# Fused attention with a gelu gate on one core: six output adds moved to GpSimd, another block order near the end, tail tasks by priority, and the last 128 queries scored in two parts of 64

## The chip, the cores and the metric

One core of a Trainium2 chip runs the whole kernel. The metric is device time in microseconds (us) of one launch. In all runs here but one it is the span of the profile plus about 1.83 us (483.73 at a span of 481.9), so spans can be used for sums.

## The reference, cut to what matters

```python
B, S, D = 1, 2048, 448             # 16 heads of 28 columns; F = 1792
xn = _layernorm(x, axis=-1)
scores = jnp.einsum("bhqd,bhkd->bhqk", q, k) * 28 ** -0.5
p = _softmax(scores, axis=-1)
s = jnp.einsum("bhqk,bhkd->bhqd", p, v).reshape(B, S, D) @ wo
g = _silu(_gelu(xn @ w1 + b1) @ w2 + b2)
return x + s * g
```

## The kernel before

The kernel has no fixed order of instructions in its text. Every operation is a task with an engine, a modelled duration and a priority; a scheduler that runs while the program is built picks, engine by engine, the next task and writes it into that engine's queue.

The work is 16 blocks: four groups of heads by four chunks of 512 queries. Within a block, TensorE forms a tile of scores (128 keys by 512 queries for one head, into the PSUM buffer `ring`), ScalarE takes its exponential into `P`, and TensorE multiplies `P` by the values into `acc`. ScalarE exponentiates three tiles at a time (1536 columns), sometimes two (1024): then VectorE computes the third, a **late tile**, with a polynomial.

```python
yield _Task(DVE, lambda eng: eng.tensor_scalar(v, lo, EXP_SC / 65536.0, None, op0=ALU.mult), ty, [tv], d0, 0.0, 4)
yield _Task(DVE, lambda eng: eng.scalar_tensor_tensor(u, v, EXP_A, v, op0=ALU.add, op1=ALU.mult),
            [tv], [tu], d1, 0.0, 4)
# ... two more steps on u and v ...
yield _Task(DVE, lambda eng: eng.scalar_tensor_tensor(pl.bitcast(dt.uint16), y, 2.0 ** -9, u,
                                                      op0=ALU.mult, op1=ALU.add),
            ty + [tu], [K.b_pl[k]], d1, 0.0, 4)          # the late tile, for TensorE
```

The five steps are L1297, L1298, L1300, L1302, L1304 before the change and L1310, L1311, L1313, L1315, L1317 after it. TensorE's value product of a late tile stands in TensorE's fixed order; if the polynomial is not done, everything behind it waits, the next scores too.

When all four groups of a chunk are done, its four output tiles of 128 queries are projected, multiplied by the gate out of PSUM and added to x:

```python
def t_oev(self, ps, tok, c, t):
    ...
    yield _Task(DVE, lambda eng: eng.tensor_tensor(o, ps, K.g_sb[:, c, t, :], ALU.mult), ..., [wr], 0.63, 0.0, 3)
    yield _Task(DVE, lambda eng: eng.tensor_tensor(o, o, K.x2[:, c, t, :], ALU.add),
                [K.b_x2[c], wr], [wr], 0.4, 0.0, 3)
```

The gate of the very last tile is made after the last exponential, on GpSimd:

```python
yield _Task(POOL, lambda eng: eng.tensor_tensor(o, sg[:, 3, :], fb[:, 3, :], ALU.mult), ..., 0.85, 0.05, 0)
yield _Task(POOL, lambda eng: eng.tensor_tensor(o, o, fb[:, 3, :], ALU.add), ..., 0.85, 0.05, 0)
```

## Time and profile before

| | before |
|---|---|
| time, median of 3 | 483.76 us (483.73 to 483.79) |
| span of the profiled run, its own time | 483.1, 484.9 us |
| exponentials of 1536 / 1024 columns on ScalarE | 249 / 100 |
| last exponential's end to last add's end | 4.47 us |
| GpSimd busy | 43.2 us (9%) |

### The profile page before, as it was taken

Reading aid. Unit: us, or ns where it says so; the run is one execution under the profiler, and the core shown is the slowest. Engines: PE = TensorE matmul, PEld = TensorE weight load, DVE = VectorE, ACT = ScalarE, POOL = GpSimd, SP = SyncE. Lnnn points to the kernel's source line nnn. Section 1 sums busy time; section 2 is a strip of 40 time slices with the busy share of each in tenths; the row PEclk is TensorE's granted clock in tenths of the full one; section 3 lists DMA queues with packets and bytes.
Section 4 is the critical chain, followed back from the end, with each engine's and each line's share of the span. In section 5 each row is a group of like instructions: output and inputs, shape, how many; then the busy total and the mean of one; then the engine's idle time right before and its main releaser. Section 6 shows DMA issues by size and latency. Waiting matters only on the chain.

```text
span 483.1 us, 10155 instructions
## 1 busy us (share of the span) xinstructions
PE 438.5 (91%) x4232; PEld 168.1 (35%) x4268; DVE 407.6 (84%) x592; ACT 468.8 (97%) x390; POOL 43.2 (9%) x77
## 2 busy tenths in 40 slices
PE   6999899998889898999989988999999999999995
PEld 5442333332223333332323343333333333333453
DVE  8946888989978989989878749899997999889785
ACT  5999999999999999999999999999999999999994
POOL 7470000000010000000101000010100100100001
PEclk9998999999999999999999999999999999999998
DMA  8501000000000000000400000000101010011011
GB/s 247 149 9 28 1 0 2 1 2 2 0 1 1 1 1 1 1 2 1 134 1 0 1 2 0 1 2 1 38 1 40 1 38 1 23 37 58 3 39 39
DMA packets 8288, 11.08 MB, mean 23 GB/s; under 512 B 1650, under 2 KB 6898, under 8 KB 8243
## 3 DMA queue, kind: packets, MB, share of 16 engines
q1 hardware_dynamic: 8098, 10.21, 7.0%
q8 instruction: 33, 0.54, 0.5%
q10 hardware_dynamic: 144, 0.23, 0.1%
q14 instruction: 13, 0.10, 0.1%
HBM read 8.61 MB, written 1.84 MB: 22 GB/s over the span
## 4 chain that ended last, share of the span: by engine, by line
ACT 45%; PE 32%; issue 17%; DVE 5%; ACTq 0%; DVEq 0%
ACT P L1160 42%; PE ring L1129 9%; PE acc L1346 6%; PE misc L1065 4%; PE acc L857 3%; PE misc L695 2%; ACT h L1044 2%; PE misc L1007 1%; PE acc L839 1%; PE misc L949 1%; PE misc L1442 1%; PE ring L1007 1%; ACT w L1080 1%; PE ring L949 1%; DVE kT L1298 0%
## 5 line engine op out<-in xcount | busy, mean ns | idle before, releaser
L1160 ACT ACTIVATE P<-ring 128x1536 bf16<-128x1536 f32 (+1 forms) x350 | 428.9, 1469 | 1.7 <-PE ring L1129 1.5
L1129 PE MATMUL ring<-qT,kT 32*128 32x512 bf16 (+2 forms) x1144 | 136.5, 360 | 26.1 <-ACT P L1160 22.0
L1346 PE MATMUL acc<-P,vaug 128*32 128x512 bf16 (+2 forms) x1074 | 95.0, 363 | 1.0 <-issue 0.5
L1129 PEld LDWEIGHTS ring<-qT,kT 32*128 32x128 bf16 x1144 | 35.5, 91 | 132.8 <-ACT P L1160 123.5
L1183 DVE TENSOR_SCALAR x_sb<-ring 128x512 int32<-128x512 f32 x68 | 46.8, 688 | 14.2 <-PE ring L1129 13.0
L1065 PE MATMUL misc<-w,h 128*128 128x448 bf16 x224 | 52.3, 355 | 0.1
L1415 POOL CAST rhi<-rc 128x16 bf16<-128x16 f32 x15 | 10.3, 686 | 402.5 <-DVE rc L1413 255.6
L857 PE MATMUL acc<-ident,zero 128*128 128x128 bf16 x516 | 44.8, 221 | 0.0
L1346 PEld LDWEIGHTS acc<-P,vaug 128*32 128x32 bf16 x1074 | 24.4, 93 | 51.0 <-issue 46.6
L857 PEld LDWEIGHTS acc<-ident,zero 128*128 128x128 bf16 x516 | 29.8, 98 | 21.3 <-issue 19.4
L1007 PE MATMUL misc<-xnT,w 128*128 128x512 bf16 x127 | 35.9, 382 | 1.3 <-issue 0.8
L990 DVE CAST h<-misc 128x512 bf16<-128x512 f32 x35 | 24.1, 688 | 8.1 <-PE misc L1007 7.0
L1304 DVE SCALAR_TENSOR_TENSOR x_sb<-x_sb,kT 128x1024 uint16<-128x1024 int32 (+1 forms) x24 | 26.7, 1111 | 0.5
L1302 DVE SCALAR_TENSOR_TENSOR kT<-kT 128x1024 f32<-128x1024 f32 (+1 forms) x24 | 26.6, 1110 | 0.5
L1298 DVE SCALAR_TENSOR_TENSOR kT<-kT 128x1024 f32<-128x1024 f32 (+1 forms) x24 | 26.5, 1104 | 0.6
L1300 DVE SCALAR_TENSOR_TENSOR kT<-kT 128x1024 f32<-128x1024 f32 (+1 forms) x24 | 26.4, 1102 | 0.2
L1065 PEld LDWEIGHTS misc<-w,h 128*128 128x128 bf16 x224 | 17.3, 97 | 23.9 <-issue 12.1
L1007 PE MATMUL ring<-xnT,w 128*128 128x512 bf16 x82 | 19.3, 380 | 2.0 <-ACT h L1044 1.6
L1298 DVE SCALAR_TENSOR_TENSOR w<-w 128x1024 f32<-128x1024 f32 (+1 forms) x18 | 20.3, 1128 | 0.3
L1304 DVE SCALAR_TENSOR_TENSOR x_sb<-x_sb,w 128x1024 uint16<-128x1024 int32 (+1 forms) x18 | 20.3, 1130 | 0.2
L1300 DVE SCALAR_TENSOR_TENSOR w<-w 128x1024 f32<-128x1024 f32 (+1 forms) x18 | 20.3, 1130 | 0.2
L1302 DVE SCALAR_TENSOR_TENSOR w<-w 128x1024 f32<-128x1024 f32 (+1 forms) x18 | 20.3, 1129 | 0.1
(154 smaller groups left out, 449.6 us busy)
## 6 DMA issues: line engine op xcount, KB each, us to landing
h<-in_A_x_dram SPq DMA_DIRECT2D x4, 448.0 KB, 3.3
w<-in_B_w_dram SPq DMA_DIRECT2D x1, 1568.0 KB, 7.3
x_sb<-in_A_x_dram SPq DMA_DIRECT2D x3, 448.0 KB, 5.2
w<-in_B_w_dram SPq DMA_DIRECT2D x1, 1344.0 KB, 9.4
out_dram<-h SPq DMA_DIRECT2D x6, 224.0 KB, 1.9
h<-in_A_wqkv_dram SPq DMA_DIRECT2D x3, 168.0 KB, 5.5
out_dram<-h SPq DMA_DIRECT2D x4, 112.0 KB, 1.7
wo<-in_A_wo_dram SPq DMA_DIRECT2D x16, 24.5 KB
```

Of the source, the lines that this page charges most:

```text
L857: ins = eng.matmul(K.acc[:, 0:128], K.zero[:, :], K.ident[:, :], start=False, stop=True, skip_group_check=True)
L990: yield _Task(DVE, lambda eng: eng.tensor_copy(dst, bank), [tok], wr, 0.69, 0.0, 2)
L1007: ins = eng.matmul(bank, K.w1[:, kt, ft * 128:(ft + 1) * 128], K.xnT[:, kt, c * 512:(c + 1) * 512], start=(kt == 0), stop=(kt == KT - 1))
L1065: ins = eng.matmul(ps, hv[:, ft, t * 128:(t + 1) * 128], K.w2[:, ft, :], start=(ft == 0), stop=(ft == FT - 1))
L1129: return eng.matmul(K.ring[:, RB[m], col:col + nq], K.kT[32 * j:32 * j + 32, g, t * 128:(t + 1) * 128], K.qT[32 * j:32 * j + 32, g, c * 51 ...
L1160: return eng.activation(K.P[:, p0:p0 + n, :], K.ring[:, b0:b0 + n, :], ACTF.Exp, scale=SM_SCALE)
L1183: yield _Task(DVE, lambda eng, m=m, i=i, half=half: eng.tensor_scalar(K.ysb[i][:, 512 * half:512 * half + 512], K.ring[:, RB[m], :], SM_SC ...
L1298: yield _Task(DVE, lambda eng: eng.scalar_tensor_tensor(u, v, EXP_A, v, op0=ALU.add, op1=ALU.mult), [tv], [tu], d1, 0.0, 4)
L1300: yield _Task(DVE, lambda eng: eng.scalar_tensor_tensor(u, u, EXP_B, u, op0=ALU.add, op1=ALU.mult), [tu], [tu], d1, 0.0, 4)
L1302: yield _Task(DVE, lambda eng: eng.scalar_tensor_tensor(u, v, EXP_D, u, op0=ALU.mult, op1=ALU.add), [tv, tu], [tu], d1, 0.0, 4)
L1304: yield _Task(DVE, lambda eng: eng.scalar_tensor_tensor(pl.bitcast(dt.uint16), y, 2.0 ** -9, u, op0=ALU.mult, op1=ALU.add), ty + [tu], [K. ...
L1346: return eng.matmul(K.acc[32 * j:32 * j + 32, q0:q0 + nq], K.vaug[:, t, 4 * g + j, :], ap[:, col:col + nq], tile_position=(0, 32 * j), sta ...
```

## The change

The intent is to empty the end. The last two blocks are both on the last chunk, so that the outputs of chunk 2 are finished a block earlier; six output adds go from VectorE to the idle GpSimd, and the gate's last add the other way; the last 128 queries are handled as two parts of 64; in the tail the scheduler looks ahead for tasks of higher priority. Small matmuls weigh less in the scheduler's count of TensorE activity, and the thresholds for late tiles were tuned again.

```diff
+GC = [(b // C, b % C) for b in range(11)] + [(3, 0), (3, 1), (3, 2), (2, 3), (3, 3)]
-THS = (..., 8.0, 8.0, 8.0, 7.0, 3.0)
+THS = (..., 7.0, 8.0, 4.0, 9.0, 3.0)
+PARTS = [(0, 128), (128, 128), (256, 128), (384, 64), (448, 64)]
+TAIL = 18
+POOL_ADD = 8
...
+            if self.exp_m >= MTOT - TAIL and E in (PE, DVE):
+                for s2, p2 in sorted(((c[0], c[1]) for c in cand), key=lambda c: c[0]):
+                    if p2[3].E == E and p2[3].prio < p[3].prio and s2 < s + p[3].dur - 0.1:
+                        s, p = s2, p2
+                        break
...
-            yield _Task(POOL, lambda eng: eng.tensor_tensor(o, o, fb[:, 3, :], ALU.add),
+            yield _Task(DVE, lambda eng: eng.tensor_tensor(o, o, fb[:, 3, :], ALU.add),
...
-        yield _Task(DVE, lambda eng: eng.tensor_tensor(o, o, K.x2[:, c, t, :], ALU.add),
-                    [K.b_x2[c], wr], [wr], 0.4, 0.0, 3)
+        E, dur = (POOL, 1.05) if POOL_ADD <= 4 * c + t < 14 else (DVE, 0.4)
+        yield _Task(E, lambda eng: eng.tensor_tensor(o, o, K.x2[:, c, t, :], ALU.add),
+                    [K.b_x2[c], wr], [wr], dur, 0.0, pr)
```

(Cut: the pieces of 64 queries, weights 0.15 and 0.3 of small matmuls, the holding back of filler matmuls before a block's copy, priorities.)

More of the change, by code (lines that the diff above doesn't have):

```diff
@@ L47 @@
 LATE_GAP, LATE_SUB = 3, 15
-THS = (8.0, 4.0, 7.0, 8.0, 4.0, 7.0, 9.0, 6.0, 6.0, 8.0, 8.0, 8.0, 8.0, 8.0, 7.0, 3.0)
-SLACKS = (6.0, 5.0, 3.0, 5.0, 2.0, 6.5, 9.0, 6.5, 3.0, 4.0, 7.0, 6.0, 8.0, 6.0, 8.0, 3.0)
+THS = (8.0, 4.0, 7.0, 8.0, 4.0, 7.0, 9.0, 6.0, 6.0, 8.0, 8.0, 7.0, 8.0, 4.0, 9.0, 3.0)
+SLACKS = (6.0, 5.0, 3.0, 5.0, 2.0, 6.5, 9.0, 6.5, 2.0, 4.0, 7.0, 6.0, 8.0, 6.0, 8.0, 3.0)
 NU = len(UNITS)
@@ L83 @@
 class _Task:
-    __slots__ = ("E", "fn", "reads", "writes", "dur", "lat", "rank")
+    __slots__ = ("E", "fn", "reads", "writes", "dur", "lat", "rank", "w")
     @property
@@ L88, in prio, with __init__ @@
         return self.rank() if callable(self.rank) else self.rank
-    def __init__(self, E, fn, reads=(), writes=(), dur=0.1, lat=0.05, prio=5):
+    def __init__(self, E, fn, reads=(), writes=(), dur=0.1, lat=0.05, prio=5, w=1.0):
         self.E, self.fn, self.reads, self.writes = E, fn, list(reads), list(writes)
-        self.dur, self.lat, self.rank = dur, lat, prio
+        self.dur, self.lat, self.rank, self.w = dur, lat, prio, w
 class _Kernel:
@@ L111, in __init__ @@
         self.pe_hist = deque()
+        self.hold = False
     def sem(self, name):
@@ L171, in put @@
         if t.E == PE:
-            self.pe_hist.append((start, start + t.dur))
+            self.pe_hist.append((start, start + t.dur * t.w))
         return h
@@ L223, in run @@
                     s = self.start_of(p[3])
-                    if s is not None:
+                    if s is not None and not (self.hold and p[3].E == PE and p[3].prio >= 90):
                         cand.append((s, p))
@@ L368, in alloc @@
         self.b_selb = B()
-        self.b_E4, self.b_on4, self.b_o4 = ([B() for _ in range(4)] for _ in range(3))
+        self.b_E4, self.b_on4, self.b_o4 = ([B() for _ in range(5)] for _ in range(3))
         self.b_rf = [B(), B()]
-        self.b_sig3, self.b_g3 = B(), B()
+        self.b_sig3, self.b_g3, self.b_g3m = B(), B(), B()
         self.banks = [(self.misc[:, :], self.b_misc), (self.acc[:, :], self.b_acc)]
@@ L403, in schedule @@
         K.late = set(MLATE)
-        K.late_left = [len([m for m in MLATE if K.sub_of(m) == b]) for b in range(NBLK + 3)]
+        K.late_left = [len([m for m in MLATE if K.sub_of(m) == b]) for b in range(NBLK + 4)]
         K.late_q = deque()
@@ L879, in f @@
             return ins
-        yield _Task(PE, f, K.b_wsq[g0:g1] + [K.b_pads], [tok], 0.15 * n + 0.1, 0.1, pr)
+        yield _Task(PE, f, K.b_wsq[g0:g1] + [K.b_pads], [tok], 0.15 * n + 0.1, 0.1, pr, 0.15)
         for b in K.b_hf[1]:
@@ L1093, in p_silu @@
             yield _Task(ACT, lambda eng: eng.activation(sg[:, 3, :], fb[:, 3, :], ACTF.Tanh, scale=0.5),
-                        [K.b_fsb[c % 2]], [K.b_sig3], 0.47, 0.0, 0)
+                        [K.b_fsb[c % 2]], [K.b_sig3], 0.87, 0.0, 0)
             yield _Task(POOL, lambda eng: eng.tensor_tensor(o, sg[:, 3, :], fb[:, 3, :], ALU.mult),
-                        [K.b_sig3, K.b_fsb[c % 2]], [K.b_h[c], K.b_g3], 0.85, 0.05, 0)
-            yield _Task(POOL, lambda eng: eng.tensor_tensor(o, o, fb[:, 3, :], ALU.add),
-                        [K.b_fsb[c % 2]], [K.b_h[c], K.b_g3], 0.85, 0.05, 0)
+                        [K.b_sig3, K.b_fsb[c % 2]], [K.b_h[c], K.b_g3m], 1.03, 0.05, 0)
+            yield _Task(DVE, lambda eng: eng.tensor_tensor(o, o, fb[:, 3, :], ALU.add),
+                        [K.b_fsb[c % 2], K.b_g3m], [K.b_h[c], K.b_g3], 0.4, 0.0, 0)
     def pieces(self, m):
@@ L1105, in pieces @@
             return b, r % 4, [(2 * (r // 4) + k, 0, 256, 256 * k) for k in range(2)], r == 31, 0
-        s, r = r // 16 - 1, r % 16
-        return b, r % 4, [(4 * (r // 4) + k, 128 * (s + 1), 128, 128 * k) for k in range(4)], r == 15, s
+        if r < 48:
+            r -= 32
+            return b, r % 4, [(4 * (r // 4) + k, 256, 128, 128 * k) for k in range(4)], r == 15, 1
+        s, r = (r - 32) // 8, r % 8
+        return b, r % 4, [(8 * (r // 4) + k, 256 + 64 * s, 64, 64 * k) for k in range(8)], r == 7, s
     def p_take(self, b):
@@ L1120, in p_scores @@
             ps = [(m,) + K.pieces(m) for m in ms]
-            for k in range(4):
+            for k in range(8):
                 for m, b, j, pc, _, _ in ps:
@@ L1125, in p_scores @@
                     t, q0, nq, col = pc[k]
-                    g, c = b // C, b % C
+                    g, c = GC[b]
                     def f(eng, m=m, t=t, j=j, g=g, c=c, q0=q0, nq=nq, col=col):
@@ L1268, in p_mlate @@
                 b, j, pc, _, _ = K.pieces(m)
-                t, g, c = pc[0][0], b // C, b % C
+                t, (g, c) = pc[0][0], GC[b]
                 yield _Task(PE, lambda eng, j=j, g=g, t=t, c=c, bank=bank: eng.matmul(
@@ L1336, in p_pv @@
             fl, rd = [], []
-            for kk in range(4):
+            for kk in range(8):
                 for m, ap, tok in src:
                     _, j, pc, _, s = K.pieces(m)
-                    g = q // 16 // C
+                    g = GC[q // 16][0]
                     if kk >= len(pc):
@@ L1366, in p_pv @@
             if end:
+                K.hold = True
                 K.spawn(K.p_epi(b) if b < NBLK - 1 else K.p_epi4(first - NBLK + 1), 0.5)
@@ L1374, in p_epi4 @@
         K = self
-        ts = ((0, 1), (2,), (3,))[s]
-        sl = slice(128 * ts[0], 128 * (ts[-1] + 1))
+        ts = ((0, 1), (2,), (3,), (4,))[s]
+        sl = slice(PARTS[ts[0]][0], sum(PARTS[ts[-1]]))
         yield _Task(DVE, lambda eng: eng.tensor_copy(K.E_sb[:, 1, sl], K.acc[:, sl]), [K.b_acc, K.b_E[1]],
-                    [K.b_E4[t] for t in ts], 0.16 + 0.13 * len(ts), 0.0, 0)
+                    [K.b_E4[t] for t in ts], 0.16 + 0.00105 * (sl.stop - sl.start), 0.0, 0)
         K.E_done = NBLK - 1 + s
+        K.hold = False
         for t in ts:
@@ L1385, in p_norm4 @@
         g, c = G - 1, C - 1
-        E, tE = K.E_sb[:, 1, 128 * t:128 * (t + 1)], K.b_E4[t]
+        q0, n = PARTS[t]
+        E, tE = K.E_sb[:, 1, q0:q0 + n], K.b_E4[t]
         bank, tok = yield ("bank", lambda: K.g_done[C - 1])
-        yield _Task(PE, lambda eng: eng.matmul(bank[:, 0:128], K.selb[:, :], E, start=True, stop=True),
-                    [tE, K.b_selb], [tok], 0.1, 0.12, 3)
-        R = K.rf[:, t % 2, :]
-        yield _Task(DVE, lambda eng: eng.reciprocal(R, bank[:, 0:128]), [tok], [K.b_rf[t % 2]], 0.96, 0.0, 1)
+        yield _Task(PE, lambda eng: eng.matmul(bank[:, 0:n], K.selb[:, :], E, start=True, stop=True),
+                    [tE, K.b_selb], [tok], 0.1, 0.12, 2 if t < 3 else 0)
+        R = K.rf[:, t % 2, 0:n]
+        yield _Task(DVE, lambda eng: eng.reciprocal(R, bank[:, 0:n]), [tok], [K.b_rf[t % 2]], 0.12 + 0.0066 * n, 0.0,
+                    1 if t < 3 else 0)
         K.banks.append((bank, tok))
-        dst = K.qT[:, g, c * 512 + 128 * t:c * 512 + 128 * (t + 1)]
+        dst = K.qT[:, g, c * 512 + q0:c * 512 + q0 + n]
         yield _Task(DVE, lambda eng: eng.tensor_tensor(dst, E, R, ALU.mult), [tE, K.b_rf[t % 2], K.b_qT[g][c]],
-                    [K.b_on4[t]], 0.3, 0.0, 1)
-        K.on4[t] = True
+                    [K.b_on4[t]], 0.16 + 0.00105 * n, 0.0, 1 if t < 3 else 0)
+        if t != 3:
+            K.on4[min(t, 3)] = True
     def p_epi(self, b):
         K = self
-        g, c = b // C, b % C
+        g, c = GC[b]
         E = K.E_sb[:, b % 2, :]
@@ L1404, in p_epi @@
         K.E_done = b
+        K.hold = False
         bank, tok = yield ("bank", lambda: K.ready([tE], 0.2))
@@ L1411, in f @@
             return ins
-        yield _Task(PE, f, [tE, K.b_bsel], [tok], 0.25, 0.1, 3)
+        yield _Task(PE, f, [tE, K.b_bsel], [tok], 0.25, 0.1, 3, 0.3)
         yield _Task(DVE, lambda eng: eng.reciprocal(K.rc[:, :], bank[:, 0:16]), [tok], [K.b_rc], 0.26, 0.0, 1)
@@ L1444, in f @@
             return ins
-        return _Task(PE, f, [K.b_wo] + [K.b_on4[t] if (g, c) == (G - 1, C - 1) else K.b_onT[g][c] for g in gs], [tok], 0.2 * len(gs) + 0.05, 0.12, prio)
+        return _Task(PE, f, [K.b_wo] + [x for g in gs for x in (([K.b_on4[t]] + K.b_on4[4:] * (t == 3)) if (g, c) == (G - 1, C - 1) else [K.b_onT[g][c]])], [tok], 0.2 * len(gs) + 0.05, 0.12, prio)
     def t_oev(self, ps, tok, c, t):
@@ L1449, in t_oev @@
         o = K.osb[:, c, t, :]
+        pr = 3 if (c, t) != (C - 1, 3) else 0
         wr = K.b_osb[c][t // 2] if c < C - 1 else K.b_o4[t]
         yield _Task(DVE, lambda eng: eng.tensor_tensor(o, ps, K.g_sb[:, c, t, :], ALU.mult),
-                    [tok, K.b_g3 if (c, t) == (C - 1, 3) else K.b_g[c]], [wr], 0.63, 0.0, 3)
-        yield _Task(DVE, lambda eng: eng.tensor_tensor(o, o, K.x2[:, c, t, :], ALU.add),
-                    [K.b_x2[c], wr], [wr], 0.4, 0.0, 3)
+                    [tok, K.b_g3 if (c, t) == (C - 1, 3) else K.b_g[c]], [wr], 0.63, 0.0, pr)
+        E, dur = (POOL, 1.05) if POOL_ADD <= 4 * c + t < 14 else (DVE, 0.4)
+        yield _Task(E, lambda eng: eng.tensor_tensor(o, o, K.x2[:, c, t, :], ALU.add),
+                    [K.b_x2[c], wr], [wr], dur, 0.0, pr)
         ov = K.out[0].rearrange("(c p t) d -> c p t d", p=128, t=4)[c]
@@ L1463, in p_out @@
         K = self
-        bank, tok = yield ("bank", lambda: K.on_done[(G - 1) * C + c] and K.g_done[c])
+        bank, tok = yield ("bank", lambda: K.on_done[GC.index((G - 1, c))] and K.g_done[c])
         ps = bank[:, 0:D]
@@ L1476, in p_last @@
         ps = bank[:, 0:D]
-        yield K.t_wo(ps, tok, c, t, (0, 1, 2), 3)
+        for g in range(G - 1):
+            yield K.t_wo(ps, tok, c, t, (g,), 3)
         yield ("until", lambda: K.on4[t])
-        yield K.t_wo(ps, tok, c, t, (3,), 3)
+        yield K.t_wo(ps, tok, c, t, (3,), 3 if t < 3 else 1)
         yield from K.t_oev(ps, tok, c, t)
```

## The prediction

> **What bounds the kernel now.** I read the page first (busy shares, then the forty slices), then ScalarE's groups by shape, then the stretches in which ScalarE was not full, then the timeline of the end. ScalarE is the bound: 97% busy, and in the slices it shows 9 from the second to the last but one.
>
> ```profile
> PE 438.5 (91%) x4232; PEld 168.1 (35%) x4268; DVE 407.6 (84%) x592; ACT 468.8 (97%) x390; POOL 43.2 (9%) x77
> ...
> ACT  5999999999999999999999999999999999999994
> ...
> PEclk9998999999999999999999999999999999999998
> ...
> L1160 ACT ACTIVATE P<-ring 128x1536 bf16<-128x1536 f32 (+1 forms) x350 | 428.9, 1469 | 1.7 <-PE ring L1129 1.5
> ```
>
> So a shorter time can come from three places only: less work on ScalarE, the 1.7 us in which its exponentials waited, and the ends (13 us before the first exponential, and everything after the last). The clock row has one 8 inside the body, in the fourth slice. Stretches of 1 us there show why: the granted TensorE clock is 0.50 for about 3.4 us, and ScalarE falls to 0.16 us busy out of 1.
>
> ```profile
> 42.00:43.00 1.00, 1.00 (x10) 0.30 (x8) 0.57 (x1) 1.00 (x2) 0.00 (x0) 1.00 0.00 0
> 43.00:44.00 1.00, 0.81 (x5) 0.13 (x2) 0.18 (x1) 1.00 (x2) 0.00 (x0) 0.59 0.06 16
> ...
> 45.00:46.00 1.00, 1.00 (x6) 0.11 (x4) 0.73 (x2) 0.89 (x1) 0.00 (x0) 0.50 0.00 0
> 46.00:47.00 1.00, 1.00 (x10) 0.28 (x7) 0.51 (x1) 0.16 (x1) 0.00 (x0) 0.70 0.00 0
> ```
>
> (Columns: stretch, its length, busy us of PE, PEld, DVE, ACT, POOL, then the clock.) The timeline has the victim: two projection matmuls take 1.03 us where the same two take 0.60 at 35.8 us, the scores behind them come late, and ScalarE waits 0.96 us.
>
> ```profile
> 44.75 1.03 PE L695 MATMUL misc<-xnT,wq 128*128 128x512 bf16 x2
> ...
> 46.84 2.79 ACT L1160 ACTIVATE P<-ring 128x1536 bf16<-128x1536 f32 x2 [0.96 <-PE ring L1129]
> ```
>
> The end, in the timeline: the last exponential (892 ns, starting at 475.57) is done at 476.46; call that A. The values product starts at A+0.24 behind three output matmuls, and the last DVE add ends at 480.93 = A+4.47; 2.17 us later the span ends (store, landing 1.7).
>
> ```profile
> 476.70 0.41 PE L1346 MATMUL acc<-P,vaug 128*32 128x128 bf16 x16
> ...
> 477.16 0.29 DVE L1377 CAST E_sb<-acc 128x128 bf16<-128x128 f32 x1 [0.27 <-PE acc L1346]
> 477.44 0.63 DVE L1451 TENSOR_TENSOR h<-ring,h 128x448 bf16<-128x448 f32 x1
> ...
> 478.06 0.96 DVE L1391 RECIPROCAL w<-ring 128x128 f32<-128x128 f32 x1
> ...
> 480.54 0.39 DVE L1453 TENSOR_TENSOR h<-h 128x448 bf16<-128x448 bf16 x1
> ```
>
> The eviction at 477.44 belongs to the tile before; the reciprocal starts 0.61 us after the accumulator copy, where the path alone needs about 0.30 (0.05 to PE, 0.22 matmul, 0.03 back).
>
> **What the Trainium skill says.** "TensorE: Matmul & The Clock Gate", section "What's actually happening": the clock is halved after a window of 3413 ns with too little activity, and restored after a busy one. The trace agrees: 0.50 from about 43.2 to 46.6, one window. Same page, "Wait — 56ns, not 53.3ns?": starts are never closer than about 25 ns, however small the matmul. This trace differs where four tiles run side by side: 32 value products of 128 columns end 0.63 us after they began, 0.22 of it latency, so 13 ns each. "VectorE: DVE Perf Modes", errata section: a fixed cost per instruction. It agrees in form: the copies take 425 ns for 256 columns and 292 for 128, so 1.04 ns a column over 159 fixed. "GPSIMD Engine Reference", 4.1: two-input operations are about twice slower than on VectorE. Here 1.03 against 0.39 us.
>
> **The change, part by part**, counted in the built order of both kernels.
>
> *Clock weights.* The scheduler adds idle-filling matmuls (three of 128 columns, 0.17 us) when it thinks PE is idle. It counted twelve one-column matmuls at 40.7 us as full work. Now they weigh 0.15, and two fillers stand just before the bad window's end, one after the small matmul at 41.44 and one before the projection at 43.24. In the window 39.76 to 43.18 the timeline has seven groups of 512 columns (side by side or alone, each 0.21 us of streaming at the 13 ns per 128 columns in four tiles that is worked out above): 1.5 us of 3.42; two fillers make 1.85. By the same count other windows with 1.6 kept the full clock (around 186 and 289 us), so I give 0.7 that the dip goes. Worth: the waits 0.96 + 0.04, and 0.09 because an exponential that follows at once starts before the one before it has ended. In all −1.05.
>
> *ScalarE's work.* VectorE takes one late tile fewer (67 against 68), so ScalarE gets one exponential of 1536 columns in place of one of 1024. The pitch of 1536 is 1.34 us, the scheduler's and the trace's step per 512 columns 0.43: +0.43, on the path.
>
> *Order of blocks.* The block of the third head group on the last chunk now comes last but one, so all outputs of chunk 2 move a block earlier: four matmuls and 1.02 us of VectorE each. Both engines have room there, ScalarE does not wait for them: 0 by itself. Six adds move from VectorE (0.39) to GpSimd (1.03): off the path, 0. Twelve fillers fewer: 0.
>
> *64-query parts.* 128 score and 128 value matmuls of 64 columns replace 64 and 64 of 128. A unit of scores becomes 24 matmuls in place of 12: at 13 ns or so, +0.2 us. It must be ready within 1.34 us of its release, with at most about 0.9 us of other PE work between: 0.4 before, some 0.65 now, hidden.
>
> *The tail, step by step from A.* One output matmul, not three, stands before the value product, and is long done: start A+0.05. 32 products: 0.63, to A+0.68. Copy of 64 columns 0.23 (159 + 64 × 1.04): 0.70 to 0.93. Sum matmul to 1.20. Reciprocal of 64: from 957 ns at 128 and 248 at 16 columns, 0.55: 1.23 to 1.78. Multiply 0.23 after the 0.10 seen before: 1.88 to 2.11. Output matmul 2.16 to 2.53; the gate's add, now on VectorE, fits below it (its GpSimd half ends near A+1.6). Eviction 2.55 to 3.18, its add to 3.60. But in the built order the previous tile's add stands after that, and so does its store: to A+3.96. Against 4.47 that is −0.51; I take −0.48, as two stores now leave 0.39 us apart.
>
> Sum: 483.76 − 1.05 + 0.43 − 0.48 = 482.66, say 482.7.
>
> **Rivals.** (1) *The dip stays or moves.* For: the fillers are small, and a re-ordered body can open another poor window. Against: the sum above, and no other dip in the body now. Then 483.76 + 0.43 − 0.48 = 483.7, no gain. (2) *PE becomes the bound in the last blocks*, if 64-column matmuls run at the page's 25 ns: a unit would take 0.6 and the last products 0.8 us. Scores would still be hidden, the tail would lose 0.3 to 0.4: 483.0. (3) *VectorE sets the end*: if the deferred add cost nothing (its store hidden), 482.3. If VectorE arrives late at the late tiles of the last block, ScalarE waits: it has about 1 us of slack there, so I hold it unlikely. (4) *New waits of ScalarE* around the moved output work: the largest PE backlog between two score units falls from 2.61 to 1.92 us by my count, which speaks against it.
>
> **Range and chances.** 0.7 for about 482.6 and 0.3 for about 483.7 (rival 1), each within some 0.4. Range 481.9 to 483.9. 2% is 9.7 us, more than all that is not ScalarE's work between first and last exponential: within 2% 0.98.
>
> **What would show it.** Clock 1.00 between 42 and 47 us and no wait of 0.96 before that exponential (clock step). 250 exponentials of 1536 and 99 of 1024 (work). Last exponential's end near 475.8. From it to the last add 3.9 to 4.0 us, the last two DVE instructions adds of 0.39. A copy of 0.23 and reciprocals near 0.55. It is wrong if the clock is 0.50 there, if a new dip or a wait of ScalarE over 0.3 us appears after 300 us, or if the last products take over 0.8 us.

## More of the kernel before

The model lets an engine's task depend on data, never on what another engine does meanwhile.

The profiled run took 484.9 us, 1.1 more than any timed run: what its trace shows need not be in the times. And one line of the groups, with GpSimd's smallest operation, has a mean of 686 ns for 16 columns (columns: busy us, mean ns, idle time before and what ended it):

```profile
L1415 POOL CAST rhi<-rc 128x16 bf16<-128x16 f32 x15 | 10.3, 686 | 402.5 <-DVE rc L1413 255.6 <-PE ring L1129 82.5 <-PE acc L1346 37.9
```

One by one these casts take from 196 to 1085 ns. The same work with the same shape, five times as long at times: something outside the instruction stretches it. (In the trace the long ones are those that start beside a step of the polynomial, as at 237.35, 1085 ns beside L1298; the short ones have no such neighbour.)

## The result, and the profile after

| | before | after |
|---|---|---|
| time, median | 483.75 us (483.66 to 483.79, 4 runs) | 488.07 us (488.33, 488.05, 488.09, 486.58) |
| span of the profiled run | 483.1 | 486.5 |
| exponentials 1536 / 1024 | 249 / 100 | 250 / 99 |
| waits of ScalarE over 0.2 us after 440 us | none | 1.94, 0.26, 0.92 |
| last exponential's end to last add's end | 4.47 | 4.39 |

The ratio is 1.0083 (95% interval 1.0063 to 1.0104). Here and below a ratio is the mean time of one kernel's runs over the mean of the other's in the same rounds, so not quite the ratio of the medians. The time is 4.3 us above before and 4.2 above the top of my range.

The page of the profile, after (share rows, the forty slices, ScalarE's main group):

```profile
PE 438.4 (90%) x4349; PEld 168.1 (35%) x4385; DVE 404.2 (83%) x579; ACT 469.6 (97%) x390; POOL 49.3 (10%) x82
...
ACT  5999999999999999999999999999999999999794
...
PEclk9999999999999999999999999999999999999799
...
L1173 ACT ACTIVATE P<-ring 128x1536 bf16<-128x1536 f32 (+1 forms) x350 | 429.6, 1459 | 4.0 <-PE ring L1142 3.7
```

(POOL 49.3 for 43.2: the adds.) The 8 of the fourth slice in the clock row is gone, and a 7 stands in both rows near the end. The timeline of ScalarE shows which exponentials waited (columns: start, length, then in brackets the idle time before and what ended it):

```profile
455.32 2.86 ACT L1173 ACTIVATE P<-ring 128x1536 bf16<-128x1536 f32 x2 [1.94 <-PE ring L1142]
458.44 1.02 ACT L1173 ACTIVATE P<-ring 128x1024 bf16<-128x1024 f32 x1 [0.26 <-PE ring L1142]
460.38 19.40 ACT L1173 ACTIVATE P<-ring 128x1536 bf16<-128x1536 f32 x15 [0.92 <-PE ring L1142]
```

All three waited for scores, so for TensorE. TensorE's timeline at that place:

```profile
451.23 0.39 PE L1142 MATMUL ring<-qT,kT 32*128 32x256 bf16 x6
453.43 0.44 PE L1359 MATMUL acc<-P,vaug 128*32 128x512 bf16 x4 [1.81 <-DVE x_sb L1317]
```

TensorE stood from 451.62 to 453.43, because the last step of a late tile (L1317) was not done. The stretches of 1 us show what followed (columns: stretch, length, busy us of PE, PEld, DVE, ACT, POOL, clock, DMA share, GB/s):

```profile
452.00:453.00 1.00, 0.00 (x0) 0.00 (x0) 0.97 (x2) 1.00 (x2) 0.00 (x0) 1.00 0.62 229
...
454.00:455.00 1.00, 1.00 (x10) 0.13 (x6) 0.22 (x1) 0.00 (x0) 0.00 (x0) 0.50 0.06 16
```

After that pause TensorE's clock was 0.50 from 453.7 to about 460.5, and six score matmuls took 0.61 us in place of 0.39; I take the 0.26 and 0.92 as the price of that. So the question is why L1317 came late. VectorE's timeline of the changed kernel, and under it GpSimd's (same columns):

```profile
442.70 0.63 DVE L1471 TENSOR_TENSOR h<-misc,h 128x448 bf16<-128x448 f32 x1 [0.99 <-POOL h L1474]
443.24 1.22 DVE L1313 SCALAR_TENSOR_TENSOR kT<-kT 128x1024 f32<-128x1024 f32 x1
444.49 1.94 DVE L1315 SCALAR_TENSOR_TENSOR kT<-kT 128x1024 f32<-128x1024 f32 x1
...
446.88 1.21 DVE L1317 SCALAR_TENSOR_TENSOR x_sb<-x_sb,kT 128x1024 uint16<-128x1024 int32 x1
448.01 1.25 DVE L1310 TENSOR_SCALAR kT<-x_sb 128x512 f32<-128x512 uint16 x1
449.19 0.61 DVE L1471 TENSOR_TENSOR h<-misc,h 128x448 bf16<-128x448 f32 x1
...
450.43 1.40 DVE L1313 SCALAR_TENSOR_TENSOR kT<-kT 128x512 f32<-128x512 f32 x1
...
452.60 0.69 DVE L1317 SCALAR_TENSOR_TENSOR x_sb<-x_sb,kT 128x512 uint16<-128x512 int32 x1
```

```profile
440.71 1.88 POOL L1474 TENSOR_TENSOR h<-h 128x448 bf16<-128x448 bf16 x1 [9.38 <-DVE h L1471]
443.40 1.94 POOL L1474 TENSOR_TENSOR h<-h 128x448 bf16<-128x448 bf16 x1 [0.81 <-DVE h L1471]
447.04 1.94 POOL L1474 TENSOR_TENSOR h<-h 128x448 bf16<-128x448 bf16 x1 [1.69 <-DVE h L1471]
449.88 1.41 POOL L1474 TENSOR_TENSOR h<-h 128x448 bf16<-128x448 bf16 x1 [0.90 <-PE acc L867]
```

Read the two side by side. A GpSimd add takes 1.03 us when it has the memory to itself; these four take 1.41 to 1.94. VectorE's L1315 takes 1.22 at this shape, L1310 0.42 and L1313 at 512 columns 0.69; the three that come second to an add take 1.94, 1.25 and 1.40: 2.26 us more. Whichever starts first keeps its length: the steps at 443.24 and 446.88, each about 0.16 us ahead of an add, take 1.22 and 1.21, and the add waits. The eviction L1471, which reads PSUM, is not longer (0.61). One more 0.99 us is lost where the eviction at 442.70 waits for an add on the same output buffer, itself late: with 1.03 us it would have ended at 441.74, about when VectorE got there (441.71).

The tail of the changed kernel, in the timeline:

```profile
480.31 1.03 POOL L1105 TENSOR_TENSOR h<-w 128x448 bf16<-128x448 bf16 x1 [4.83 <-ACT w L1103]
...
480.48 0.95 DVE L1411 TENSOR_TENSOR qT<-E_sb,w 128x64 bf16<-128x64 bf16 x1
...
481.35 0.55 DVE L1407 RECIPROCAL w<-ring 128x64 f32<-128x64 f32 x1
...
483.48 0.69 DVE L1474 TENSOR_TENSOR h<-h 128x448 bf16<-128x448 bf16 x2
```

The multiply of 64 columns should take 0.23. It took 0.95 and ended 0.09 after GpSimd's L1105. The last reciprocal waits behind it.

### The profile page after: what moved, and what is told of

Same layout as the page of the kernel before. It is cut to its first block, busy times and chain, and to the rows that moved or that the text cites. A ratio compares the mean times of both kernels' runs of the same rounds, so it can differ in the third digit from the quotient of the medians.

```text
span 486.5 us, 10389 instructions
## 1 busy us (share of the span) xinstructions
PE 438.4 (90%) x4349; PEld 168.1 (35%) x4385; DVE 404.2 (83%) x579; ACT 469.6 (97%) x390; POOL 49.3 (10%) x82
## 3 DMA queue, kind: packets, MB, share of 16 engines
HBM read 8.61 MB, written 1.84 MB: 21 GB/s over the span
## 4 chain that ended last, share of the span: by engine, by line
ACT 43%; PE 30%; issue 17%; DVE 7%; DMA 1%; POOL 0%; SPq 0%; ACTq 0%; DVEq 0%; POOLq 0%
ACT P L1173 40%; PE ring L1142 9%; PE acc L1359 6%; PE misc L1075 5%; PE acc L867 2%; ACT h L1054 2%; PE misc L1017 1%; PE misc L705 1%; DMA h<-in_A_wqkv_dram 1%; DVE x_sb L1317 1%; PE misc L959 1%; PE ring L1017 1%; DVE kT L1315 1%; DVE kT L1313 1%; DVE h L1471 1%
## 5 line engine op out<-in xcount | busy, mean ns | idle before, releaser
L1142 PE MATMUL ring<-qT,kT 32*128 32x512 bf16 (+3 forms) x1208 | 137.1, 352 | 26.3 <-ACT P L1173 22.4
L1359 PE MATMUL acc<-P,vaug 128*32 128x512 bf16 (+3 forms) x1139 | 95.3, 354 | 2.9 <-DVE x_sb L1317 1.8
L1315 DVE SCALAR_TENSOR_TENSOR kT<-kT 128x1024 f32<-128x1024 f32 (+1 forms) x22 | 26.5, 1205 | 0.4
L1313 DVE SCALAR_TENSOR_TENSOR kT<-kT 128x1024 f32<-128x1024 f32 (+1 forms) x22 | 26.4, 1201 | 0.3
L1311 DVE SCALAR_TENSOR_TENSOR kT<-kT 128x1024 f32<-128x1024 f32 (+1 forms) x22 | 25.6, 1165 | 0.5
L1317 DVE SCALAR_TENSOR_TENSOR x_sb<-x_sb,kT 128x1024 uint16<-128x1024 int32 (+1 forms) x22 | 25.7, 1169 | 0.3
L1317 DVE SCALAR_TENSOR_TENSOR x_sb<-x_sb,w 128x1024 uint16<-128x1024 int32 (+1 forms) x18 | 20.3, 1130 | 0.2
L1313 DVE SCALAR_TENSOR_TENSOR w<-w 128x1024 f32<-128x1024 f32 (+1 forms) x18 | 20.3, 1129 | 0.2
L1315 DVE SCALAR_TENSOR_TENSOR w<-w 128x1024 f32<-128x1024 f32 (+1 forms) x18 | 20.3, 1128 | 0.1
```

The costliest lines, as they stand in the source:

```text
L1142: return eng.matmul(K.ring[:, RB[m], col:col + nq], K.kT[32 * j:32 * j + 32, g, t * 128:(t + 1) * 128], K.qT[32 * j:32 * j + 32, g, c * 51 ...
L1313: yield _Task(DVE, lambda eng: eng.scalar_tensor_tensor(u, u, EXP_B, u, op0=ALU.add, op1=ALU.mult), [tu], [tu], d1, 0.0, 4)
L1359: return eng.matmul(K.acc[32 * j:32 * j + 32, q0:q0 + nq], K.vaug[:, t, 4 * g + j, :], ap[:, col:col + nq], tile_position=(0, 32 * j), sta ...
```

## The experiments

**Theory**: a GpSimd operation and a late-tile step of VectorE that both read SBUF shut each other out. The Trainium skill has this, "SBUF — State Buffer", section "SBUF: two separate sides": the two engines share a pair of ports, "whichever of {DVE op in a 2-port perf mode, or with two SBUF inputs (only against a GpSimd op that reads SBUF); GpSimd op} starts first gets the pair for the whole instruction; the other fully blocks". I had not used it. (Four of the five steps have two SBUF inputs. L1310 has one; its 0.42 us at 512 and 0.69 at 1024 columns are half the other steps' time per column, which fits the 2-port mode, but no run shows its mode.) **Rivals**: the new order alone (block order, waits of the shared output buffer) makes VectorE late; TensorE's clock comes first and the waits follow; or any busy GpSimd does it. The runs came in three groups, each on a chip of its own: e1 to e4 (before: 483.62), e5 to e8 (before: 483.81), e9 to e12 (before: 483.57).

### e1: the adds hardly read anything

```diff
+        w = 8 if E == POOL else D
-        yield _Task(E, lambda eng: eng.tensor_tensor(o, o, K.x2[:, c, t, :], ALU.add),
+        yield _Task(E, lambda eng: eng.tensor_tensor(o[:, 0:w], o[:, 0:w], K.x2[:, c, t, 0:w], ALU.add),
```

Same order on every engine as after (in the traces, all 390 ScalarE, 579 VectorE and 82 GpSimd operations); the outputs are wrong.

> The changed kernel with the same order of instructions on every engine, but GpSimd's six output adds touch 8 columns instead of 448 (six output tiles are wrong on purpose). Port theory (GpSimd's adds and VectorE's two-input SBUF instructions keep each other waiting, the late tile comes late, TensorE stands in its queue behind it, its clock halves): VectorE's polynomial steps near 440 to 453 us go back to 1.22 and 0.69 us (from 1.94 and 1.40), no wait of an exponential over 0.3 us after 440 us, clock 1.00 from 440 to 470, about 3.1 us less than the changed kernel: 485.0 us, span of the profile near 483.4. Rival A (the new dip of the clock comes from the held and fewer fillers and the block order, GpSimd is a bystander): the dip at 453 to 460 stays, 487.5 to 488.1. Rival B (VectorE has too much work before that tile even at full speed): the wait shrinks from 1.94 but stays over 0.5 us.

Measured: **484.51 us** (484.39, 485.3, 484.42, 484.6), ratio to before 1.0021 (1.0006 to 1.0036). In its timeline ScalarE's exponentials run unbroken from 410.53 to the last:

```profile
410.53 65.29 ACT L1173 ACTIVATE P<-ring 128x1536 bf16<-128x1536 f32 x52
...
442.30 1.11 POOL L1475 TENSOR_TENSOR h<-h 128x8 bf16<-128x8 bf16 x1 [0.83 <-DVE h L1471]
```

Against its own runs of before that is +0.89 in place of +4.32: 3.4 us are the adds' work, not the order, and the first rival falls. The clock is 1.00 from 448 to 464 us with the same filler matmuls, so the second falls too. The second line is a gift: an add of **8 columns** (0.20 us alone) still takes 1.11 us, since it must wait for VectorE's step of 1.22 that began before it.

### e2: the adds on VectorE again

```diff
-POOL_ADD = 8
+POOL_ADD = 99
```

> The changed kernel with all output adds on VectorE (0.39 us each), scheduled anew; ScalarE gets one more 512-column step (251 exponentials of 1536). Port theory: no wait after 440 us, no dip there; against the changed kernel -3.1 +0.43, so about 485.4 us, span near 483.8. Rival A: a dip near 453 us all the same, over 487. Rival B: VectorE's 1.6 us more of adds make the late tile late again, a wait of 1 to 2 us stays.

Measured: **485.01 us** (485.05, 484.97, 485.07, 484.66), ratio 1.0025 (1.0009 to 1.0042); no wait of ScalarE after 440 us, clock 1.00 there; correct. The scheduler found room for one late tile less (251 and 98), which costs another 0.43. The remedy works, but does not make the change pay.

### e3: only the weights of small matmuls, on the kernel before

```diff
-            self.pe_hist.append((start, start + t.dur))
+            self.pe_hist.append((start, start + t.dur * t.w))
```

> The kernel before with only the new weights of small matmuls in the scheduler's activity count (21 more filler matmuls, nothing else moves on any engine). If the weights alone remove the dip at 43 us: clock 1.00 from 42 to 47 us, the wait of 0.96 gone, 1.05 us less: 482.7. Rival (the early dip went for another reason, the weights do nothing): 483.7 with the dip; or the fillers delay scores elsewhere: new waits of ScalarE, 483 to 485.

Measured: **483.74 us** (483.94, 483.73, 483.57, 483.75) against 483.62, ratio 1.0002. The profile has no dip at 43 us; but by their spans and clocks neither had the kernel before in its timed runs: 481.7 to 481.9 us at a mean clock of 0.997 to 1.000, the profiled one 483.1 at 0.993 (they left no trace). This term of my sum is worth 0.

### e4: only the six adds on GpSimd, on the kernel before

```diff
+        E, dur = (POOL, 1.05) if 8 <= 4 * c + t < 14 else (DVE, 0.4)
```

> The kernel before with only the six output adds on GpSimd; ScalarE's work unchanged, blocks in the old order. Port theory: VectorE's two-input steps beside the adds (457 to 466 us) take 1.2 to 1.9 us in place of 0.69, GpSimd's adds 1.4 to 1.9 in place of 1.03; whether the time grows depends on the slack of the late tile there (about 0.9 us): 483.5 to 485.5. Rival A (GpSimd is a bystander): VectorE's durations unchanged, 483.75 within 0.3.

Measured: **484.39 us** (484.39, 484.37, 484.39, and one of 486.22 with the same span of 482.4), ratio 1.0024 (1.0007 to 1.0042); correct. Late-tile steps are stretched here too (L1298 and L1304 take 1.40 in place of 0.69 at 458.7 and 462.0), but ScalarE has no new wait: in this order the late tile has room. The loss is in the tail. An add delays GpSimd's two gate operations, and the second now meets the last multiply (timeline of e4):

```profile
477.60 1.03 POOL L1097 TENSOR_TENSOR h<-h,w 128x448 bf16<-128x448 bf16 x1
...
477.99 0.78 DVE L1394 TENSOR_TENSOR qT<-E_sb,w 128x128 bf16<-128x128 bf16 x1
```

The multiply is 0.29 alone; from the last exponential to the last add it is 4.95 us in place of 4.47. That +0.48 is most of the +0.77.

### e5: no GpSimd in the tail

```diff
 POOL_ADD = 99
-            yield _Task(POOL, lambda eng: eng.tensor_tensor(o, sg[:, 3, :], fb[:, 3, :], ALU.mult), ...
-            yield _Task(DVE, lambda eng: eng.tensor_tensor(o, o, fb[:, 3, :], ALU.add), ...
+            yield _Task(DVE, lambda eng: eng.scalar_tensor_tensor(o, sg[:, 3, :], 1.0, fb[:, 3, :],
+                                                                  op0=ALU.add, op1=ALU.mult), ..., 0.63, 0.0, 0.5)
```

> e2_adds_on_vector (485.01 us) with one thing more taken off GpSimd: the gate of the last tile is one VectorE step (add one, multiply: 0.62 us as for the other tiles) in place of GpSimd's multiply (1.03) and VectorE's add (0.39). In e2 the first 64-column multiply of the tail, L1411, took 0.95 us beside GpSimd's L1105, the second, alone, 0.23. Blocking theory: the first multiply falls to 0.23 too, the second reciprocal starts 0.7 earlier, the 0.62 step fits into the 0.76 us between the last multiply and the last eviction, so the time is 484.35 (-0.65). Rival, the multiply is long because of what feeds it (E_sb copied just before): it stays 0.95 and the time 485.0. Correct outputs; the body up to the last exp is that of e2.

Measured: **484.57 us** (484.55, 484.56, 484.7, 484.57, 485.28), ratio 1.0019 (1.0005 to 1.0033); correct. In its timeline:

```profile
477.14 0.22 DVE L1410 TENSOR_TENSOR qT<-E_sb,w 128x64 bf16<-128x64 bf16 x1
```

The first multiply is 0.22, so its 0.95 was the port. But the tail is only 0.37 shorter than in e2 (3.95 against 4.32), not 0.65: behind the short multiply the reciprocal waits 0.16 for TensorE, loses an overlap of 0.08, and the 0.62 step ends just too late, so the last eviction starts 0.11 after it could.

### e6 and e7: what has to be read to block

In the changed kernel, same order, the six adds become a fill with a constant (e6) or a copy of `x2` (e7). Both are wrong in those tiles. (The comparison with the reference accepted e7: its tolerance does not notice the attention term missing in six tiles, so it is no proof of correctness.)

```diff
-        yield _Task(E, lambda eng: eng.tensor_tensor(o, o, K.x2[:, c, t, :], ALU.add),
+        yield _Task(E, lambda eng: (eng.memset(o, 0.5) if E == POOL else ...        # e6
+        yield _Task(E, lambda eng: (eng.tensor_copy(o, K.x2[:, c, t, :]) if E == POOL else ...   # e7
```

> The changed kernel with the same order on every engine; GpSimd's six adds become fills of the same 128x448 outputs with a constant, which write SBUF and read nothing (wrong in those outputs on purpose). If what blocks is reading (GpSimd's and VectorE's reads of SBUF exclude each other), VectorE's polynomial steps near 444 to 451 us keep 0.69 and 1.22, no ScalarE wait over 0.3 after 440, and the time is that of e1: 484.5. Rival, any busy GpSimd or its writing does it: steps of 1.4 to 1.9 us again and 486.5 to 488.

> As e6, but GpSimd copies x2 into the output: one SBUF operand is read in place of two (wrong on purpose in the six adds). If any read of SBUF by GpSimd blocks VectorE's two-operand steps, some of these are stretched by up to the copy's own length (a copy of 448 columns is not measured yet; an estimate from the adds is 0.5 to 1.0 us), and the time is between 484.8 and 488. If only GpSimd's two-operand reads block, nothing is stretched: 484.5.

Measured: e6 **484.58 us** (484.57 to 484.66), e7 **484.67 us** (484.41 to 484.75). In e6's timeline a fill lies fully beside a polynomial step, and both have their own length:

```profile
445.25 1.22 DVE L1317 SCALAR_TENSOR_TENSOR x_sb<-x_sb,kT 128x1024 uint16<-128x1024 int32 x1
...
445.39 0.47 POOL L1474 MEMSET h<- 128x448 bf16 x1 [2.45 <-DVE h L1471]
```

In e7's timeline the copies, 0.56 us alone, take up to 1.49, and three VectorE steps are longer by 0.24, 0.36 and 0.24:

```profile
446.13 1.49 POOL L1474 COPY h<-h 128x448 bf16<-128x448 bf16 x1 [1.67 <-DVE h L1471]
...
447.12 0.78 DVE L1310 TENSOR_SCALAR kT<-x_sb 128x512 f32<-128x512 uint16 x1
...
470.83 0.56 POOL L1474 COPY h<-h 128x448 bf16<-128x448 bf16 x1 [1.79 <-DVE h L1471]
```

So reading blocks, one operand or two, and writing alone does not block the two-input steps: "any busy GpSimd" falls. (No fill met the one-input step L1310, and in each meeting the VectorE step was first; that the fill kept its 0.47 is what shows it free.) And a delay costs nothing until it exceeds the room. On the time scale of the changed kernel, the late tile is done at 450.67 in e1 (450.37 plus 0.30, the difference in start), TensorE is free for it at 451.62: 0.95 us of room (0.74 within e1's own trace, 450.37 against 451.11). In its own trace e7's tile is done at 451.44 and TensorE is free for it at 451.46: just in time, and e7 is as fast as e6. After the change it was done at 453.29, 2.62 later than in e1 (the stretches of 2.26 and the wait of 0.99, less what VectorE's own pauses took up), and TensorE stood 1.81.

### e9, e10, e11: the parts of the tail, one at a time, on e5

```diff
-PARTS = [(0, 128), (128, 128), (256, 128), (384, 64), (448, 64)]      # e9: one part of 128 again
+PARTS = [(0, 128), (128, 128), (256, 128), (384, 128)]
-                    [K.b_x2[c], wr], [wr], dur, 0.0, pr)               # e10: adds of the last chunk first
+                    [K.b_x2[c], wr], [wr], dur, 0.0, 0 if c == C - 1 else pr)
-GC = [...] + [(3, 0), (3, 1), (3, 2), (2, 3), (3, 3)]                  # e11: block order of before
+GC = [(b // C, b % C) for b in range(NBLK)]
```

> e5_gate_on_vector (484.57 us, ratio 1.0019, from the last exp to the end of the last add 3.94 us) with the last 128 queries in one part again; the body to the last exp is the same (251 and 98). In the tail the last copy covers 128 columns after a longer wait for the value product (in the kernel before 0.70 after the last exp), then the gate (0.62), a reciprocal of 0.96 in place of 0.55, multiply, eviction, one add (t=2's add moves ahead): copy ends at 0.99, gate 1.5, reciprocal 2.45, multiply 2.74, eviction ends 3.9, add 4.3. Expected if the split is worth what the tail's sum says: 484.95 (+0.35). Rival, the split is worth nothing, as it brings t=2's add to the very end (0.30): 484.6 or less.

> e5_gate_on_vector with one priority changed: the add of the third 128 queries (t=2) goes before the last reciprocal in place of after the last add. The end loses 0.30 (the second of two adds that took 0.69), the last reciprocal starts later by what the add (0.39) overlaps of its wait for TensorE (0.16). Expected 484.4 (-0.1 to -0.2). Rival: the add lies on the chain of the last reciprocal with its full 0.39, and the time is 484.6 or more.

> e5_gate_on_vector with the block order of the kernel before: ScalarE has 250 exps of 1536 columns and 99 of 1024 (one 512-column piece less: -0.43), but the outputs of chunk 2 come a block later, and another eviction and add (0.55 and 0.30 to 0.39) fall behind the last exp. If the new block order pays by emptying the tail: from the last exp to the end 4.8 to 4.9 in place of 3.94, time 485.0 (+0.45). Rival, the late evictions find room beside the last reciprocals: 484.1 (the -0.43 alone).

| | time, median | ratio (95%) | last exp to last add | last exp to span's end | so the part undone is worth, at the span's end |
|---|---|---|---|---|---|
| e5 | 484.57 | 1.0019 (1.0005 to 1.0033) | 3.95 | 6.31 | |
| e9 | 484.46 | 1.0013 (0.9999 to 1.0027) | 4.11 | 6.26 | +0.05 for the 64-query parts |
| e10 | 484.04 | 1.0005 (0.9991 to 1.0019) | 3.70 | 5.86 | −0.45 more to be had by order |
| e11 | 484.67 | 1.0020 (1.0004 to 1.0035) | 4.92 | 7.09 | −0.78 for the block order |

(Cut in e9's edit: the pieces, and the priority of the sum matmul.) e9 to e11 ran on another chip than e5, whose kernel before was 0.24 slower, so I compare the ends of the profiles. The block order pays, as it keeps an eviction and an add out of the tail; but with it the tuned thresholds let VectorE take fewer late tiles, one less than in e11 and two less than before, and that gives back 0.43 or 0.86. The 64-query parts gain nothing, as e9's rival said. Before the last add they save 0.16, half of the 0.35 that I had expected, since they bring the second add to the very end; and the store takes that back. In every run whose last two stores are issued 0.38 us apart (e5 among them) the span ends 2.36 to 2.37 us after the last add; where the last store stands alone it is 2.15 to 2.17 (e9, e10). So e10 gains twice, 0.25 by the add and 0.20 by the store, where I had expected 0.1 to 0.2 in all.

### e8 and e12: a version that beats both

All adds and the last gate on VectorE, block order of before, 64-query parts, and thresholds for late tiles found by building many schedules.

```diff
-THS = (..., 9.0, 6.0, 6.0, 8.0, 8.0, 7.0, 8.0, 4.0, 9.0, 3.0)
+THS = (..., 10.0, 6.0, 10.0, 8.0, 7.0, 10.0, 9.0, 9.0, 10.0, 6.0)      # e12; e8: an earlier find
```

(Cut: a second list of thresholds, the look-ahead on TensorE alone, and the gate's priority, 4 in e8 and 0.5 in e12.)

> A version meant to beat both: block order of the kernel before, all adds and the last gate on VectorE (nothing of GpSimd beside the late tiles' steps but the small rhi/rlo casts), 64-query parts and look-ahead (TensorE alone) kept, THS and SLACKS searched anew by building many schedules (247 exps of 1536 columns and 102 of 1024, before 249 and 100). Two fewer 512-column pieces on ScalarE are -0.86 us of its work; the tail is about as long as before (4.4 to 4.5 after the last exp). Expected 482.8 to 483.2, before 483.7. Rival: more late tiles load VectorE, a value product waits for it, and ScalarE waits 0.5 to 2 us: 483.7 or above.

> e8_tuned (482.81, ratio 0.9987, its undisturbed runs 482.7) with THS and SLACKS searched further: 246 exps of 1536 columns and 103 of 1024, one 512-column piece less on ScalarE (-0.43), the tail unchanged. Expected 482.3 to 482.5. Rival: VectorE has no room left for the 79th late tile, a value product waits, and the time is 482.8 or above; or TensorE's clock halves after a wait, as in two of the five runs of e8 (483.96).

Measured: e8 **482.81 us** (483.96, 482.74, 483.96, 482.81, 482.7), ratio 0.9987 (0.9975 to 1.0). e12 **481.65 us** (481.65, 481.79, 481.51, 481.88, 481.5), ratio 0.9956 (0.9944 to 0.9969); both correct. e12 is 1.9 us faster than its own runs of before, and so some 6.2 faster than after (−1.9 against +4.3). It has 246 exponentials of 1536 and 103 of 1024, three pieces of 512 columns less than before (−1.29); a wait of 0.25 at 315 us is gone, and the tail is 3.92 (−0.55); its two stores end 0.2 later. That makes −1.9.

e8's profiled run, one of its two longer ones (483.96), shows the same port in a third place. A GpSimd operation of **16 columns**, 0.22 us alone, meets a polynomial step; TensorE waits for its result, and half clock follows from 454 to about 457.3 (timeline of e8):

```profile
452.74 1.20 POOL L1434 TENSOR_TENSOR rlo<-rc,rhi 128x16 bf16<-128x16 f32 x1
...
454.00 0.30 PE L1443 MATMUL misc<-ident,rhi 128*32 128x128 bf16 x4 [0.87 <-POOL rlo L1434]
```

e12 has this meeting as well, with the same 0.87, but no dip in its profile.

## Why the prediction was wrong

- **The step that failed** is "Six adds move from VectorE (0.39) to GpSimd (1.03): off the path, 0." I counted an engine's time as its own. Measured: with all but 8 columns of each add taken away (e1) 3.4 us less. They did not stay off the path: three VectorE steps that came second to an add lost 2.26 us, a late tile came 2.62 late, TensorE stood 1.81 and ScalarE waited 3.12 in all. In the old order the same six adds cost 0.77 (e4), so the size depends on the room. Rival 3 had the mechanism (VectorE late at a late tile) and about the right room ("about 1 us of slack": 0.74 to 0.95), but no reason why VectorE should be late, and named the last block; the tile was the last of the block before it. The order of events is stretch, late tile, idle TensorE, half clock, so the clock is a consequence. Most of the 1.94 comes before it; the 0.26, the 0.92 and some 0.6 of the 1.94 come by it (an estimate: from the held value product to the next scores TensorE needed 1.84 us, in e1 about 1.2).
- **Clock weights, −1.05: the dip did go, the gain was 0** (e3). The dip was in the profiled run and not in the timed ones, and the 1.1 us between the two times said so before I began.
- **The tail, −0.48: it became −0.08, and with the store +0.13.** The value product was faster than I worked out (0.42 in place of 0.63: I had kept the 13 ns of a 128-column product for one of 64), the copy (0.23) and reciprocals (0.55) were as said. But the multiply took 0.95 in place of 0.23, by the same port (0.22 in e5). And the two stores 0.38 us apart cost 0.21, for which my step from −0.51 to −0.48 allowed 0.03. Of the parts, the block order was the large one (0.78, in my text "0 by itself"), and the 64-query parts gained nothing (−0.16 and +0.21).
- **ScalarE's work, +0.43: right.** 250 and 99. From first to last exponential e1 is 0.70 longer than e3: this 0.43, a new wait of 0.12 at 372 us, and 0.20 by which the last exponential's record is longer (1081 ns in place of 881), which I can't explain.
- **64-column pieces: right.** 24 score matmuls took 0.41, no longer than 12 of 128 columns before (0.40), so not even the +0.2 that I had allowed, and no score unit was late by them; rival 2 falls.
- **The sum.** After against e3, by the profiles: +4.37 from the first to the last exponential (0.70 as in e1, 3.67 from the three waits of 3.12 and the overlaps lost around them), −0.08 in the tail, +0.21 in the stores: +4.50, timed +4.32.

Left open: one of the four runs after took 486.58 at a higher mean clock (0.996 against 0.991). It probably had less of the half clock; no trace of it was taken. How far blocking would change with other data types I did not try.

## What to carry to other kernels

Moving work from VectorE to an idle GpSimd is not free: if both read SBUF, the one that comes second may wait for the whole of the other, so a 0.39 us add moved away can cost VectorE more than it saves. Before such a move, look in the profile for a small GpSimd operation whose single durations differ several times over, and look which VectorE steps will lie beside the moved ones and how much room the path behind them has. Count the end to the last store's landing, not to the last add. And before taking a wait in a trace as a gain to be had, check that the profiled run is as fast as the timed ones.

## What the Trainium skill lacked or had wrong

- "SBUF — State Buffer", "SBUF: two separate sides", had the cause. Agreeing: an 8-column add took 1.11 us (0.20 alone), a 64-column multiply 0.95 (0.22 alone), and a fill that reads nothing kept its length beside a two-input step (0.47 beside 1.22). It gives no durations of two compute instructions that meet: here each late-tile step that came second to an add took 0.71 to 0.83 us more.
- "GPSIMD Engine Reference", 4.1, says that two-input operations are about twice slower on GpSimd (0.39 against 1.03 us here). That section does not add (other parts of the page do) that VectorE pays as well: 2.26 us over three steps for four adds, and an operation of 16 columns 1.20 in place of 0.22.
- "Perfetto Trace Analysis", "GPSIMD Engine Instruction", says that GpSimd instructions that read no tensor have a single point in time reported. The six fills of e6 have a length: 471 ns in the mean.
- "TensorE: Matmul & The Clock Gate", "Wait — 56ns, not 53.3ns?", puts a floor of about 25 ns between starts, and does not say how this counts where tiles of the array work side by side. In the changed kernel's trace, score matmuls of 64 columns on neighbouring tiles start 3 to 4 ns apart, those on the same tile about 29 (about 56 at 128 columns): 24 took 0.41 us in all, and 32 value products of 64 columns 0.42, latency included.
